# A transformer layer on one core: opening by halves, a mixer lead of two blocks, sums added ahead of weight fills

## The chip, the cores and the metric

The kernel runs on one core of one Trainium2 chip. The metric is device microseconds (us) of that core for one execution. Engines are PE (TensorE, matrix products), DVE (VectorE), ACT (ScalarE), POOL (GpSimd) and SP (SyncE, which here only issues transfers, "DMAs"). Each has its own queue of instructions and works through it in order; between engines only semaphores hold.

## The reference

One layer on 2048 tokens of width 1024, in float32: a pre-norm attention with a compressive memory over four segments of 512 tokens, and a pre-norm MLP.

```python
for s in range(N):                                   # N = 4 segments, H = 32 heads of 32
    logits = einsum("bhqd,bhkd->bhqk", qs, ks) * scale + mask
    a_dot = einsum("bhqk,bhkd->bhqd", softmax(logits), vs)
    pq = phi(qs)                                     # phi(t) = t + 1 if t > 0 else exp(t)
    num, den = einsum("bhld,bhde->bhle", pq, M), einsum("bhld,bhd->bhl", pq, z)[..., None] + 1e-6
    outs.append(g * num / den + (1.0 - g) * a_dot)   # g = sigmoid(beta), per head
    M, z = M + einsum("bhld,bhle->bhde", phi(ks), vs), z + phi(ks) summed over tokens
h = x + concat(outs) @ wo                            # q, k, v are layernorm(x) @ wq, wk, wv
out = h + gelu(layernorm(layernorm(h)) @ w1 + b1) @ w2 + b2   # w1: 1024 x 3584
```

## The kernel before

**Arithmetic.** Every float32 operand of a product is cut into a rounded high part (a copy, to the type f32r) and a low part (a subtraction); a product is three matmuls: high x high, high x low, low x high. Names end in h and l (`yh`, `yl`, `wh`, `wl`, `zh`, `zl`). The copy is nearly always on ACT, the subtraction on DVE or POOL. Tokens are worked on in two halves of 1024, each of two segments of 512 ("sl" 0 and 1).

**The run of one half.**
1. `ln1` normalises 4 tiles of 128 tokens a segment and turns them (PE transposes into `pt`, L142, L254). Its statistics come from DVE, its factors v and nb from POOL (`ln_scale`, `ln_offset`), the scaling xt from ACT. In half 0 the first segment is done by `opening` (L208 on), whose instructions are bound to the order they are written in (`in_order`), with the first weight blocks of wk, wq and wv.
2. `attention` goes over 8 groups of 4 heads and the two segments. `dense` makes keys `kps`, queries `qps` and values `vps` (L114 to L116); the four heads of the group and segment before (`heads`: scores `pqk` L497, exp L506, norm L513, transposes `ppt` L529, values `po` L549) are interleaved with it. With the first `dense` of a half, ln1 of its second segment is interleaved, so many of its steps for each step of `dense` as a ratio says.
3. The last heads run beside the first segment's product with wo (`wo_first`). Meanwhile `load_o` (L634 to L639) loads the second segment's attention outputs (`orr`) and cuts them (`oh`, `ol`), as a side run of which `PD` steps go before the first.
4. `wo_second` and `ln2` finish h and its double norm z; the normed tiles are turned. `ln2_combined` makes, from the second segment's tiles, sums and differences of token blocks (B22, T1 to T4, b12) in four steps a tile.
5. `Mixer`: the product with w1 is done by a scheme of seven products on 2x2 blocks. Its `lead` (L885 on) does, for each of 14 pairs of blocks (HP), `c1(j)`, 12 matmuls whose sum is saved as p (L896), and `c2(j)`, 12 more on top into the same bank of PSUM, of which ACT then makes gelu. Order on PE: c1(0), then for each j c1(j+1), c2(j). `begin` loads the first weights (`wx`; halves of two neighbouring blocks in one tile), which `upper` and `lower` cut on ACT and DVE. `ln2_combined` is interleaved with the lead at 0.4 of a step a PE step (3 matmuls); behind it `mp` is opened and the first weights of the pairs are fetched. Then the pairs (`Mixer.pair`, products `bps` and `dps`) are run. Both `lead` and pairs are bound to the written order.

In half 0, ln1 of half 1's first segment is interleaved with the last nine pairs, at 0.16.

**Second.** Behind half 1's pairs comes the product with w2 for all tokens, again by seven products, in jobs of 21 matmuls (`po`, L1201). For job n, `work` loads rows, makes sums (POOL), cuts the operands of job n + 2 (`prep`, L1143), and fills weight slots that are due (`fill_up`: POOL sum, ACT copy, DVE subtraction L1074). `add` then adds the product to the outputs `c` (DVE, L1211), and frees its bank.

**What sets the order.** Instructions are ordered on each engine as they are written or, outside `in_order`, by a scheduler that follows priorities from the order of writing and the dependencies. `behind`, and `add_manual_dep` with NOSYNC, hold one instruction behind another of its engine. A tile pool's tag with n buffers makes the n+1st use wait for the release of the first. PSUM has the tags d (3 banks), qk (2), pt (2) and av (1).

Of the kernel before, what the change touches and what calls it, by code (L numbers as in the profile page):

```python
# [3 lines left out]

# [21 lines left out]
NG = 8  # L26
HT = 1024
NT = HT // P
RA, RH, RS, PD, PS = 1.3, 14, 0.7, 16, 3
# [13 lines left out]
def build(tc, x, wq, wk, wv, wo, beta, w1, b1, w2, b2, out):  # L43
# [88 lines left out]
    def ln_offset(pool, m, r):  # L132
        nb = pool.tile([P, 1], F32, name="nb", bufs=4)
        nc.gpsimd.tensor_scalar(nb, m, -1.0, r, op0=ALU.mult, op1=ALU.mult)
        return nb
# [59 lines left out]
    def ln1(half, sl, delay=0):  # L195
# [8 lines left out]
        acts["y", sl] = yh, yl = seg_tiles(sl, "y")  # L204

        def take(name):
            return psum.tile([P, 512], F32, tag="av", name=name, bufs=1)

        yield from ln_tiles(lnp, xs, yh, yl, False, act=True,
                            fold=lambda src, t4: ln_transpose(lnp, src, yh, yl, t4, take))  # L210

    def opening():

        xs = [lnp.tile([P, D], F32, tag="ln", name="xt", bufs=4) for _ in range(4)]
        for t, xt in enumerate(xs):
            nc.sync.dma_start(xt, x[0, t * P:(t + 1) * P, :])
        raws, ws = {}, {}

        def load(n, w):
            raws[n] = wp.tile([P, DC, P], F32, tag="wr", name="wr", bufs=2)  # L220
            nc.sync.dma_start(raws[n], w[:, 0:P].rearrange("(c p) n -> p c n", p=P))

        def halves(n, hi_eng):
            ws[n] = [wp.tile([P, DC, P], F32R, tag=f"w{x_}", name=f"w{x_}", bufs=3) for x_ in "hl"]
            (nc.vector.tensor_copy if hi_eng == "vector" else nc.scalar.copy)(ws[n][0], raws[n])
            for k in (slice(0, 4), slice(4, 8)):
                nc.gpsimd.tensor_tensor(ws[n][1][:, k], raws[n][:, k], raw(ws[n][0])[:, k], op=ALU.subtract)
# [12 lines left out]

        def normal(t):
            m, r = scales[t][:2]
            if t < 3:
                nc.scalar.activation(xs[t], xs[t], AF.Identity, bias=scales[t][2], scale=r)
            else:
                nc.vector.tensor_scalar(xs[t], xs[t], m, r, op0=ALU.subtract, op1=ALU.mult)

        def turn(t):
            folds[t] = []
            for c in range(2):  # L250
                pt = ps_dense("pt").rearrange("p (a b) -> p a b", a=4)
                for i in range(4):
                    k = 4 * c + i
                    nc.tensor.transpose(pt[:, i, :], xs[t][:, k * P:(k + 1) * P], ident)  # L254
# [42 lines left out]
    def attention(half, first):  # L297
        ab = tc.alloc_tile_pool(name=f"ab{half}", bufs=1, reuse_waits="tile")
        acts["ab"] = ab
        mask = ab.tile([P, 512], F32, name="mask")  # L300
        quiet = behind if first else lambda op: op
        quiet(nc.gpsimd.memset(mask, 0.0))
        nc.gpsimd.affine_select(mask[:, 384:512], mask[:, 384:512], pattern=[[-1, P]],
                                compare_op=ALU.is_ge, fill=-1e9 / SCALE, base=0, channel_multiplier=1)
        mz_flat = acts["mz"] = ab.tile([P, NG * 132 + 96], F32, name="MZ")
        MZ = mz_flat[:, :NG * 132].rearrange("p (g e) -> p g e", g=NG)
        ZC = acts["mz"][:, NG * 132:NG * 133]
        if half == 0:
            quiet(nc.gpsimd.memset(mz_flat, 0.0))
        else:  # L310
            nc.sync.dma_start(mz_flat, mz_dram)
# [54 lines left out]
        def dense(g, sl, ws, u):  # L366
            s = 2 * half + sl
            behind = acts.pop("late", iter(()))
            kps = ps_dense("kps")
            for c in project(ws["k"], sl, "kps", kps):  # L370
                if c >= 2:
                    next(behind, None)
                yield
# [261 lines left out]
    def load_o(half, sl, g, tp):  # L635
        oh, ol = o_tiles(half, sl)
        orr = tp.tile([P, 512], F32, tag="tmp", name="orr", bufs=5)
        nc.sync.dma_start(orr, o_dram[2 * half + sl][g])
        split(None, orr, oh[:, g, :], ol[:, g, :], hi_eng="scalar", lo_eng="vector" if g % 2 else "gpsimd")  # L639
# [113 lines left out]
    def ln2_combined(half, hts):  # L753
# [9 lines left out]
        def fold(src, t4):  # L763
# [14 lines left out]
            def halves(name, w, lo):  # L778
                nc.scalar.copy(at[name][0], w)
                lo.tensor_tensor(at[name][1], w, raw(at[name][0]), op=sub)  # L780

# [5 lines left out]
            nc.gpsimd.tensor_tensor(t1, b12, raw(at["B11"][0]), op=sub)  # L787
            nc.gpsimd.tensor_tensor(t1, t1, raw(at["B11"][1]), op=sub)
            yield
            pt = turned(1)  # L790
            nc.scalar.copy(at["B22"][0], pt)
            nc.vector.tensor_tensor(t3, pt, b12, op=sub)
            nc.vector.tensor_tensor(at["B22"][1], pt, raw(at["B22"][0]), op=sub)
            yield
            nc.vector.tensor_tensor(t2, pt, t1, op=sub)
            nc.gpsimd.tensor_tensor(t4s, raw(at["B21"][0]), t2, op=sub)
            nc.gpsimd.tensor_tensor(t4s, t4s, raw(at["B21"][1]), op=ALU.add)
            halves("T3", t3, nc.vector)
            halves("T1", t1, nc.vector)
            yield  # L800
            halves("T2", t2, nc.vector)
            yield
            halves("T4", t4s, nc.gpsimd)
# [26 lines left out]
    class Mixer:  # L830
# [22 lines left out]
        def begin(self):  # L853
# [3 lines left out]
            def load(j):  # L857
                if j < HP:
                    raws[j] = wr = wp.tile([P, DC, P], F32, tag="wr", name="wx", bufs=2)
                    for k, b in ((0, j + 1), (4, j)):  # L860
# [4 lines left out]
            def upper(j):  # L865
                if j < HP:
                    k = slice(0, 4) if j < 0 else slice(4, 8) if j == HP - 1 else slice(0, 8)
# [9 lines left out]

            load(-1)
            load(0)
            upper(-1)  # L880
            lower(-1)
            load(1)
            self.early = load, upper, lower, left

        def lead(self):  # L885
# [19 lines left out]
            for j in (0, 1):  # L905
                upper(j)
                lower(j)
                if j == 0:
                    load(2)
            self.step = -1  # L910
            yield from c1(0)
            for j in range(HP):
# [3 lines left out]
                yield from c1(j + 1)  # L916
# [69 lines left out]
    class Second:  # L986
# [148 lines left out]
        def prep(self, n):  # L1135
            if n < len(self.jobs):
# [37 lines left out]
        def work(self, n):  # L1174
# [5 lines left out]
            self.prep(n + 2)  # L1180
            self.fill_up(n)
# [48 lines left out]
    first = opening()  # L1230
    for half in range(2):
        acts["zt"] = zt = tc.alloc_tile_pool(name=f"zt{half}", bufs=1, side="right")
        rest = attention(half, None if half else first)
# [67 lines left out]
        if half == 0:  # L1301
# [3 lines left out]
            interleave(chain(*(mixer.pair(j) for j in range(HP - 9, HP))), ln1(1, 0, 2), 0.16)  # L1305
# [4 lines left out]
        else:  # L1310
# [3 lines left out]
            for j in range(HP):  # L1314
# [3 lines left out]
                for n, _ in enumerate(mixer.pair(j)):  # L1318
# [44 lines left out]
```

## Time and profile before

| | |
|---|---|
| median of 3 runs | 2350.75 us (2349.97 to 2351.35) |
| profiled execution | 2351.56 us |
| its span in the trace | 2349.8 us |
| PE busy | 2287.8 us (97%) |
| DVE, ACT, POOL busy | 1577.1, 1231.1, 1090.0 us |
| mean granted clock of PE | 0.995 of full speed |

The span is what the trace covers; the rest of an execution's time lies around it. A row of a timeline is start, length, engine, line, operation, out<-in, shapes and number, with the idle time of the engine before it and what ended it in square brackets. Matmuls overlap in a queue, so the start-to-start step of two matmuls, not the length, is what one costs.

### The profile page before, as it was taken

The page shows a single profiled execution, that of the slowest core. Times are in us where ns is not written, and L with a number is a line of the kernel's source. Part 1 is how long each engine was busy: PE and PEld are TensorE (multiplying, and loading weights), DVE is VectorE, ACT ScalarE, POOL GpSimd, SP SyncE. Part 2 cuts the span into 40 slices and gives each one's busy share as a digit, 9 for nine tenths or more (in the row PEclk, how much of TensorE's full clock was granted, in tenths as well). Part 3 has the DMA queues.
Part 4 walks back from the last instruction along what each step waited for, and adds up shares of the span by engine and source line. Part 5 has one row for each costly group of instructions (what it writes and reads, how often), then busy time and mean ns, then how long its engine had stood idle before and what let it go on. Part 6 is the DMA issues. An engine that isn't in the chain of part 4 may idle for free.

```text
span 2349.8 us, 35272 instructions
## 1 busy us (share of the span) xinstructions
PE 2287.8 (97%) x11745; PEld 1893.0 (81%) x11745; DVE 1577.1 (67%) x3252; ACT 1231.1 (52%) x2555; POOL 1090.0 (46%) x1093
## 2 busy tenths in 40 slices
PE   7999999999999999999999999999999999999999
PEld 5888888877878887888888887878887878887887
DVE  5777777775655565777777776564566786567653
ACT  5777777775453444777777776353343223223221
POOL 4445555554253443555555545262444564155430
PEclk9999999999999999999999999999999999999999
DMA  5333333344365654433333334456567975577762
GB/s 167 98 90 91 86 85 86 88 123 161 129 192 166 193 166 136 120 85 86 86 86 86 89 103 146 142 177 196 157 178 256 353 256 189 168 241 228 251 219 93
DMA packets 322575, 355.36 MB, mean 151 GB/s; under 512 B 26174, under 2 KB 218714, under 8 KB 322394
## 3 DMA queue, kind: packets, MB, share of 16 engines
q1 hardware_dynamic: 259226, 316.40, 44.8%
q10 hardware_dynamic: 63168, 36.71, 5.2%
q8 instruction: 93, 1.52, 0.3%
q14 instruction: 88, 0.72, 0.1%
HBM read 226.59 MB, written 76.09 MB: 129 GB/s over the span
## 4 chain that ended last, share of the span: by engine, by line
PE 73%; DVE 7%; ACT 6%; DMA 5%; POOL 5%; issue 3%; SPq 0%; ACTq 0%; POOLq 0%; DVEq 0%
PE po L1201 21%; PE bps L826 8%; PE dps L826 5%; PE ppt L529 5%; PE po L549 5%; PE pqk L497 3%; PE vps L114 2%; PE vps L115 2%; PE vps L116 2%; PE kps L114 2%; PE kps L116 2%; PE kps L115 2%; PE cps L826 2%; PE qps L115 2%; PE qps L114 2%
## 5 line engine op out<-in xcount | busy, mean ns | idle before, releaser
L513 POOL TENSOR_SCALAR pr<-pr,nm,gate 128x128 f32<-128x128 f32 (+3 forms) x512 | 321.6, 637 | 361.9 <-DVE nm L510 286.1
L506 ACT ACTIVATE pr<-pr,mx 128x256 f32<-128x256 f32 (+3 forms) x512 | 287.6, 562 | 162.5 <-DVE mx L498 159.6
L536 DVE TENSOR_TENSOR ptl<-ppt,pth 128x512 fp32r<-128x512 f32 (+1 forms) x384 | 227.6, 600 | 77.9 <-ACT pth L531 72.9
L498 DVE CUSTOM_DVE_ANT_0 pr<-pqk,mask 128x256 f32<-128x256 f32 (+3 forms) x512 | 243.0, 484 | 38.6 <-PE pqk L497 36.4
L529 PE MATMUL ppt<-ident,pr 128*128 128x128 f32 x1280 | 223.5, 277 | 5.8 <-DMA orr<-o_dram 3.8
L531 ACT CAST pth<-ppt 128x512 fp32r<-128x512 f32 (+1 forms) x384 | 194.1, 517 | 37.6 <-PE ppt L529 31.5
L1211 DVE TENSOR_TENSOR c<-c,po 128x512 f32<-128x512 f32 x160 | 105.4, 683 | 143.8 <-PE po L1201 143.5
L529 PEld LDWEIGHTS ppt<-ident,pr 128*128 128x128 f32 x1280 | 164.2, 140 | 37.2 <-DVE ptl L536 6.4
L91 POOL TENSOR_TENSOR wl<-wr,wh 128x1024 fp32r<-128x1024 f32 x53 | 126.9, 2394 | 87.3 <-DVE wh L88 33.6
L497 PE MATMUL pqk<-ks,qs 96*128 96x256 f32 (+3 forms) x512 | 161.8, 316 | 0.5 <-DVE mx L498 0.5
L549 PE MATMUL po<-ptl,vs 128*64 128x512 f32 (+3 forms) x512 | 154.9, 312 | 4.6 <-DVE ptl L536 4.4
L549 PE MATMUL po<-pth,vs 128*64 128x512 f32 (+3 forms) x512 | 156.8, 328 | 1.5 <-ACT pth L531 1.5
L1201 PE MATMUL po<-w2h,zh 128*128 128x512 f32 x378 | 120.8, 389 | 0.0
L934 POOL TENSOR_TENSOR s<-r 128x512 f32<-128x512 f32 x28 | 42.6, 1520 | 160.7 <-DVE sa L950 102.6
L497 PEld LDWEIGHTS pqk<-ks,qs 96*128 96x128 f32 x512 | 96.4, 188 | 22.3 <-DVE mx L498 0.9
L1071 POOL TENSOR_TENSOR w2r<-w2r 128x512 f32<-128x512 f32 x54 | 88.7, 1654 | 54.3 <-DMA w2r<-in_B_w 36.3
L826 PE MATMUL bps<-zh,sa 128*128 128x512 f32 x336 | 110.8, 391 | 1.6 <-DVE u L964 1.6
L826 PE MATMUL bps<-zh,sb 128*128 128x512 f32 x336 | 110.9, 391 | 0.9 <-DVE u L976 0.9
L114 PE MATMUL kps<-yh,wh 128*128 128x512 f32 x256 | 108.5, 424 | 0.9 <-ACT yh L144 0.8
L114 PE MATMUL vps<-yh,wh 128*128 128x512 f32 x256 | 108.9, 426 | 0.2 <-ACT omt L479 0.2
L114 PE MATMUL qps<-yh,wh 128*128 128x512 f32 x256 | 107.7, 421 | 0.0
L1201 PE MATMUL po<-w2h,hl 128*128 128x512 f32 x322 | 103.0, 389 | 2.5 <-DVE c L1211 2.5
(237 smaller groups left out, 6700.7 us busy)
## 6 DMA issues: line engine op xcount, KB each, us to landing
hr<-h_dram SPq DMA_DIRECT2D x112, 448.0 KB, 5.1
w2r<-in_B_w SPq DMA_DIRECT2D x122, 256.0 KB, 4.2
r<-in_B_w SPq DMA_DIRECT2D x56, 512.0 KB, 4.2
h_dram<-ht ACTq DMA_DIRECT2D x84, 256.0 KB, 3.7
ks<-kh SPq DMA_DIRECT2D x256, 64.0 KB, 2.0
qs<-qh SPq DMA_DIRECT2D x256, 64.0 KB, 2.0
wr<-in_A_wo SPq DMA_DIRECT2D x32, 512.0 KB, 3.9
wx<-in_B_w SPq DMA_DIRECT2D x56, 256.0 KB, 3.9
```

What stands on the lines that cost most here:

```text
L114: nc.tensor.matmul(ps, ah, bh, start=first, stop=False)
L115: nc.tensor.matmul(ps, ah, bl, start=False, stop=False)
L497: nc.tensor.matmul(pqk[:, :n], u["qs"][j][:, i * P:(i + 1) * P], u["ks"][j][:, 0:n], start=True, stop=True)
L498: nc.vector.tensor_tensor_reduce(out=st["pr"][:, offs[i]:offs[i] + n], in0=pqk[:, :n], in1=mask[:, 512 - n:512], op0=ALU.add, op1=ALU.min, ...
L506: nc.scalar.activation(pi, pi, AF.Exp, bias=mx[:, i:i + 1], scale=-1.0, accum_out=mx[:, 4 + i:5 + i])
L513: nc.gpsimd.tensor_scalar(pi, pi, nm[:, 4 + k:5 + k], gate[:, 1, 4 * g + j:4 * g + j + 1], op0=ALU.mult, op1=ALU.mult)
L529: nc.tensor.transpose(ppt[:, o:o + P], pr[:, offs[i] + jk * P:offs[i] + (jk + 1) * P], ident)
L531: nc.scalar.copy(pth[:, base:base + w], ppt[:, :w])
L536: nc.vector.tensor_tensor(o, x0, x1, op=ALU.subtract)
L549: nc.tensor.matmul(po[:, P * jk:], v, st[part][:, koff[jk]:koff[jk] + w], start=(jk, part) == (0, "pth"), stop=(jk, part) == (2, "ptl"))
L826: nc.tensor.matmul(ps, x_[:, c, :], y_[:, c, :], start=first and c == 0 and n == 0, stop=last and c == 3 and n == 2, skip_group_check=True)
L1201: nc.tensor.matmul(ps, x_[:, k], y_[k], start=opens and k == 0 and i == 0, stop=closes and k == self.KP - 1 and i == 2, skip_group_check=True)
```

## The change

- Opening: the attention pool, with the memsets of its mask and of MZ, is made before it. Tile 0 of x is loaded in two halves. The transposes use the banks of qk and pt. The first key block `kps` is made in `opening`, in two halves of 256 tokens (`keys`), the first six of the first half's eight steps before the last tile is turned. POOL's second half of q's low part, wv's load and v's low part go into ln1 (`rest`, by `aside`), v's held behind POOL's nb. ln1 of the second segment runs at 1.6 instead of 1.1.
- `load_o` of the second segment: the copy oh is held behind the last matmul written, and `PD` is 20 instead of 16.
- `ln2_combined` takes six steps a tile instead of four, and its first subtraction of t1 goes from POOL to DVE, which reads PSUM.
- `lead` runs c1 two blocks ahead of c2, and loads and cuts accordingly.
- ln1 of half 1's second segment is begun in the last pairs of half 0 (its first three steps), at 0.17 instead of 0.16.
- In `Second`, `add` of job n goes ahead of `fill_up`, and the operands of job 2 are cut in the last pair.

```diff
-RA, RH, RS, PD, PS = 1.3, 14, 0.7, 16, 3
+RA, RH, RS, PD, PS = 1.3, 14, 0.7, 20, 3
-        nc.gpsimd.tensor_scalar(nb, m, -1.0, r, op0=ALU.mult, op1=ALU.mult)
+        acts["nb"] = nc.gpsimd.tensor_scalar(nb, m, -1.0, r, op0=ALU.mult, op1=ALU.mult)
...
     def opening():
-        for t, xt in enumerate(xs):
-            nc.sync.dma_start(xt, x[0, t * P:(t + 1) * P, :])
+        for k in (slice(0, 512), slice(512, 1024)):
+            nc.sync.dma_start(xs[0][:, k], x[0, 0:P, k])
+        for t in range(1, 4):
+            nc.sync.dma_start(xs[t], x[0, t * P:(t + 1) * P, :])
...
-                pt = ps_dense("pt").rearrange("p (a b) -> p a b", a=4)
+                pt = psum.tile([P, 512], F32, tag=("qk", "pt")[c], name="pt", bufs=2).rearrange("p (a b) -> p a b", a=4)
...
+        kps = ws["kps"] = ps_dense("kps")
+
+        def keys(i, cs):
+            n = slice(256 * i, 256 * i + 256)
+            for c in cs:
+                mm3(kps[:, n], ws["k"][0][:, c, :], ws["k"][1][:, c, :], yh[:, c, n], yl[:, c, n], c == 0, c == DC - 1)
...
-            halves("k", "vector")
+            upper("k", "vector")
+            under("k", 0)
+            under("k", 1)
             turn(1)
             lower(1, 0)
             normal(3)
             turn(2)
             lower(2, 0)
+            keys(0, range(6))
             turn(3)
             lower(3, 0)
             lower(3, 1)
-            halves("q", "scalar")
-            load("v", wv)
-            halves("v", "scalar")
+            keys(0, range(6, DC))
+            upper("q", "scalar")
+            under("q", 0)
+            keys(1, range(DC))
+
+        def rest(t):
+            if t == 0:
+                under("q", 1)
+                load("v", wv)
+                upper("v", "scalar")
+            elif t < 3:
+                tc.add_manual_dep(under("v", t - 1).ins, acts["nb"].ins.name, NOSYNC, reason="program order")
...
-                    interleave(d, ln1(half, 1), 1.1)
+                    interleave(d, acts.pop("ahead") if half else ln1(0, 1, aside=ws.pop("rest")), 1.1 if half else 1.6)
...
-        split(None, orr, oh[:, g, :], ol[:, g, :], hi_eng="scalar", lo_eng="vector" if g % 2 else "gpsimd")
+        hi, lo = oh[:, g, :], ol[:, g, :]
+        op = nc.scalar.copy(hi, orr)
+        if sl == 1:
+            tc.add_manual_dep(op.ins, acts["mm"].ins.name, NOSYNC, reason="program order")
+        (nc.vector if g % 2 else nc.gpsimd).tensor_tensor(lo, orr, raw(hi), op=ALU.subtract)
...
-            nc.gpsimd.tensor_tensor(t1, b12, raw(at["B11"][0]), op=sub)
+            nc.vector.tensor_tensor(t1, pt, raw(at["B11"][0]), op=sub)
+            yield
             nc.gpsimd.tensor_tensor(t1, t1, raw(at["B11"][1]), op=sub)
-            yield
             pt = turned(1)
...
-                    h, l, _ = left[j - 1]
+                    h, l, _ = left[j - 2]
...
-                yield from c1(j + 1)
+                yield from c1(j + 2)
                 lower(j + 2)
                 yield from c2(j)
...
             self.prep(n + 2)
+            self.add(*got)
             self.fill_up(n)
...
-                got = self.product(n)
-                self.work(n)
-                self.add(*got)
+                self.work(n, self.product(n))
...
-            interleave(chain(*(mixer.pair(j) for j in range(HP - 9, HP))), ln1(1, 0, 2), 0.16)
+            acts["ahead"] = ln1(1, 1)
+            interleave(chain(*(mixer.pair(j) for j in range(HP - 9, HP))),
+                       chain(ln1(1, 0, 2), islice(acts["ahead"], 3)), 0.17)
...
+                    if (j, n) == (HP - 1, 14):
+                        second.prep(2)
```

More of the change, by code (lines that the diff above doesn't have):

```diff
@@ L3 @@
 from functools import partial
+from itertools import islice
 import concourse.bass as bass
@@ L193, in seg_tiles, with ln1 @@
         return h, l
-    def ln1(half, sl, delay=0):
+    def ln1(half, sl, delay=0, aside=None):
         xs = []
@@ L295, in load_block, with attention_pool, attention @@
         return wh, wl
[L297 to L302, printed above, removed]
+    def attention_pool(half):
+        ab = acts["ab"] = tc.alloc_tile_pool(name=f"ab{half}", bufs=1, reuse_waits="tile")
+        mask = acts["mask"] = ab.tile([P, 512], F32, name="mask")
+        nc.gpsimd.memset(mask, 0.0)
         nc.gpsimd.affine_select(mask[:, 384:512], mask[:, 384:512], pattern=[[-1, P]],
                                 compare_op=ALU.is_ge, fill=-1e9 / SCALE, base=0, channel_multiplier=1)
-        mz_flat = acts["mz"] = ab.tile([P, NG * 132 + 96], F32, name="MZ")
-        MZ = mz_flat[:, :NG * 132].rearrange("p (g e) -> p g e", g=NG)
+        acts["mz"] = ab.tile([P, NG * 132 + 96], F32, name="MZ")
+        if half == 0:
+            nc.gpsimd.memset(acts["mz"], 0.0)
+        else:
+            nc.sync.dma_start(acts["mz"], mz_dram)
+    def attention(half, first):
+        ab, mask = acts["ab"], acts["mask"]
+        MZ = acts["mz"][:, :NG * 132].rearrange("p (g e) -> p g e", g=NG)
         ZC = acts["mz"][:, NG * 132:NG * 133]
[L308 to L311, printed above, removed]
         def tmp(name):
@@ L368, in dense @@
             behind = acts.pop("late", iter(()))
[L369 to L372, printed above, removed]
-                yield
+            kps = ws.pop("kps", None)
+            if kps is None:
+                kps = ps_dense("kps")
+                for c in project(ws["k"], sl, "kps", kps):
+                    if c >= 2:
+                        next(behind, None)
+                    yield
             kh, kl = tmpr("kh"), tmpr("kl")
@@ L776, in turned @@
                 return pt
-            def halves(name, w, lo):
-                nc.scalar.copy(at[name][0], w)
-                lo.tensor_tensor(at[name][1], w, raw(at[name][0]), op=sub)
+            hi = lambda name, w: nc.scalar.copy(at[name][0], w)
+            lo = lambda name, w, eng: eng.tensor_tensor(at[name][1], w, raw(at[name][0]), op=sub)
             b12, t1 = pair("b12t1")
@@ L859, in load @@
                     raws[j] = wr = wp.tile([P, DC, P], F32, tag="wr", name="wx", bufs=2)
[L860 removed]
+                    for k, b in ((0, j + 2), (4, j)):
                         if 0 <= b < HP:
@@ L903, in c2 @@
                 self.out(j, 0, ps)
-            for j in (0, 1):
+            for j in (-1, 0):
                 upper(j)
                 lower(j)
-                if j == 0:
-                    load(2)
+                load(j + 2)
             self.step = -1
             yield from c1(0)
+            left.pop(-2)
+            upper(1)
+            yield from c1(1)
+            left.pop(-1)
+            lower(1)
             for j in range(HP):
@@ L1135, in prep @@
         def prep(self, n):
-            if n < len(self.jobs):
+            if n < len(self.jobs) and n not in self.hl:
                 src, b = self.srcs.pop(self.jobs[n])
@@ L1172, in ahead, with work @@
                         self.out(*self.at(p, w))
-        def work(self, n):
+        def work(self, n, got):
             late, self.later = self.later, []
@@ L1228, in zx_tile @@
         return acts["zt" if n == 3 else "zx"].tile([P, 4, 512], F32R, tag=f"t{x_}{n}", name=f"z{x_}{n}")
-    first = opening()
     for half in range(2):
         acts["zt"] = zt = tc.alloc_tile_pool(name=f"zt{half}", bufs=1, side="right")
-        rest = attention(half, None if half else first)
+        attention_pool(half)
+        first = None if half else opening()
+        rest = attention(half, first)
         hts = [lnp.tile([P, D], F32, tag="ln", name="ht0", bufs=4) for _ in range(4)]
```

47 lines of the change are left out of this document (29 added, 18 removed).

## The prediction

> **What bounds the kernel now.** I read the page's totals first, the waits of PE second, the granted clock in short windows third, and the instructions around each wait last.
>
> ```profile
> span 2349.8 us, 35272 instructions
> PE 2287.8 (97%) x11745; PEld 1893.0 (81%) x11745; DVE 1577.1 (67%) x3252; ACT 1231.1 (52%) x2555; POOL 1090.0 (46%) x1093
> ```
>
> PE is the bound: it is busy 2287.8 of 2349.8 us and no other engine passes 67%. The change leaves the multiplications as they are, so it can win only the 62 us in which PE stands still, and whatever PE does slowly. The waits of PE name the first:
>
> ```profile
> PE pt L254 <- ACT xt L244: 8.5, 1, 8.5
> PE cps L826 <- ACT p L896: 7.9, 7, 2.8
> PE po L1201 <- DVE c L1211: 7.9, 3, 3.3
> PE pt L142 <- ACT xt L163: 7.1, 2, 5.2
> PE ppt L529 <- DMA orr<-o_dram: 3.8, 1, 3.8
> PE cps L826 <- DVE wl L876: 1.3, 2, 0.7
> ```
>
> The columns are total us, number, longest. The 8.5 at L254 is the load and norm of the first tokens, which stays. The other five make 28.0 us, all at places that the change touches. Slow work is the second part. In these windows (start:end, length, busy time of PE, PEld, DVE, ACT and POOL, granted clock, DMA share, GB/s) PE is busy at about half clock behind a wait:
>
> ```profile
> 30.00:34.00 4.00, 4.00 (x14) 3.03 (x13) 1.29 (x2) 2.20 (x3) 0.26 (x1) 0.54 0.22 51
> 536.00:538.00 2.00, 1.56 (x4) 0.71 (x3) 2.00 (x6) 1.98 (x7) 1.27 (x2) 0.50 0.71 244
> 540.00:542.00 2.00, 2.00 (x10) 1.80 (x9) 1.91 (x5) 1.28 (x4) 1.17 (x4) 0.50 0.00 0
> 676.00:680.00 4.00, 4.00 (x13) 3.21 (x12) 4.00 (x3) 2.96 (x5) 3.11 (x2) 0.65 0.30 85
> 1566.00:1570.00 4.00, 4.00 (x12) 3.12 (x11) 4.00 (x3) 3.02 (x5) 3.19 (x3) 0.57 0.36 112
> 924.00:928.00 4.00, 4.00 (x15) 3.08 (x14) 1.52 (x3) 3.08 (x4) 2.73 (x9) 0.57 0.62 209
> 1816.00:1818.00 2.00, 1.14 (x5) 0.99 (x6) 2.00 (x4) 0.07 (x1) 0.00 (x0) 1.00 0.78 215
> ```
>
> A window costs its length times one minus its clock: 1.8 us at 30, 3.0 over 536 to 542, 1.4, 1.7 and 1.7 at 676, 1566 and 924. That is 9.6 us. The last row shows that not every wait brings it (the 3.3 us wait for c ends at 1816.9, at full clock). So 37.6 us lie open, and beside them what the opening could start earlier.
>
> **Opening.**
>
> ```profile
> 16.90 0.50 PE L114 MATMUL kps<-yh,wh 128*128 128x512 f32 x1
> 23.02 0.39 PE L114 MATMUL qps<-yh,wh 128*128 128x512 f32 x1
> 28.84 1.12 PE L142 MATMUL pt<-ident,xt 128*128 128x128 f32 x4 [5.21 <-ACT xt L163]
> 18.47 2.54 POOL L227 TENSOR_TENSOR wl<-wr,wh 128x512 fp32r<-128x512 f32 x2 [4.11 <-ACT wh L225]
> 21.30 2.53 POOL L227 TENSOR_TENSOR wl<-wr,wh 128x512 fp32r<-128x512 f32 x2 [0.28 <-ACT wh L225]
> 23.77 0.53 POOL L302 MEMSET mask<- 128x512 f32 x1
> 24.23 1.06 POOL L309 MEMSET MZ<- 128x1152 f32 x1
> 27.24 0.51 POOL L134 TENSOR_SCALAR nb<-mv,v 128x1 f32<-128x1 f32 x2
> 154.22 0.28 PE L497 MATMUL pqk<-ks,qs 96*128 96x256 f32 x1
> 154.33 0.40 PE L114 MATMUL qps<-yh,wh 128*128 128x512 f32 x1
> 154.57 0.40 PE L115 MATMUL qps<-yl,wh 128*128 128x512 f32 x1
> ```
>
> The 24 key matmuls run from 16.90 to 23.02, because they wait for all four token tiles. The change makes them 48 of 256 columns. A 256-column matmul holds PE from 154.22 to 154.33, 0.11 us, and one of 512 from 154.33 to 154.57, 0.24 (0.23 on the mean of a long run), so the halves cost nothing in sum (24 x 0.11 = 2.6 us each). Eighteen of the first half's run before tile 3 is turned, in PE's present gaps; behind the folded last tile, at about 16.9 us, stand 6 + 24 matmuls, 3.4 us. The queries then start near 20.4 instead of 23.0: 2.6 us won. [...]
>
> POOL today does two weights' low halves (5.1 us of work from 18.47 to 23.8) and both memsets before the norm's factors nb at 27.24, and PE waits 5.21 us for the normalised xt. Afterwards the memsets come first, when POOL has little to do, and the second half of q and all of v go between and behind the nb's. nb then needs only q's first half (1.27 us, from 18.5) and its own steps: near 22, with xt normalised at 23.5. PE still meets three small waits there, which I put at 3.5 us together by following the new order on ACT and DVE (an estimate from the durations quoted), so 1.7 of 5.2 is won. The slow window goes: 1.8. Sum 6.1; I take 6. Ends: 3 (the new waits are as long as the old one), 8.5 (they and the rest of the waits go). The two loads of tile 0 count nothing: its statistics need both halves. On SP the wv load and ln1's tile loads change places with nothing that is waited for.
>
> **o loads held back (the later order of orr and oh).**
>
> ```profile
> 529.79 0.62 ACT L90 CAST oh<-orr 128x512 fp32r<-128x512 f32 x1 [3.41 <-DMA orr<-o_dram]
> 525.05 1.92 SPq L638 DMA_DIRECT2D orr<-o_dram  x4
> 534.38 0.44 PE L529 MATMUL ppt<-ident,pr 128*128 128x128 f32 x2 [3.79 <-DMA orr<-o_dram]
> ```
>
> ACT stands 3.41 us before a copy of orr, whose load SP issued at 525.05 behind wo's weights; behind it wait an exp and the copy of ppt, and PE stands 3.79. In the new order the first copy comes 20 ACT instructions later, behind those, some 10 us on. Its added order edge is behind a matmul already queued, and what stands behind it on ACT is the next head's exp, by then with its data loaded. I take the whole wait and its slow window, 3.8 + 3.0 = 6.8, rounded 7. Lower end 3.5: the wait returns by half at a later copy. Half 1 shows no such wait, and gains nothing.
>
> **Mixer lead and combined operands.**
>
> ```profile
> 674.67 0.50 PE L826 MATMUL cps<-zh,wh 128*128 128x512 f32 x1 [2.77 <-ACT p L896]
> 673.51 0.62 ACT L779 CAST zh<-b12t 128x512 fp32r<-128x512 f32 x1 [0.17 <-POOL b12t L788]
> L787 POOL TENSOR_TENSOR b12t<-b12t,zh 128x512 f32<-128x512 f32 x4 | 5.6, 1408 | 0.9 <-ACT b12t L786 0.9
> L795 DVE TENSOR_TENSOR t2t<-pt,b12t 128x512 f32<-128x512 f32 x3 | 2.1, 687 | 4.2 <-POOL b12t L788 4.2
> ```
>
> Today c2(j) needs the p copy of c1(j), and one product (c1(j+1), 12 matmuls of 0.23, 2.7 us) stands between them. ACT makes the p copy in its order, behind casts that wait for POOL (the cast at 673.51). With c1(j+2) ahead, three products, 8.2 us, cover the same copy, and each weight pair is due one block later. The waits of cps for p (7.9) and wl (1.3) should go, with the slow windows at 676 and 1566 (1.4 + 1.7): 12.3 in both halves. Against that, an extra half-size cast and subtraction per half beside PE's own start, and a bank must be free two blocks earlier: gelu of j-2, behind the same ACT queue, has some 5.4 us (two products) before PE needs it. Six steps a token move t1's first subtraction from POOL (1.41 us, 4 a half) to DVE from PSUM (0.69, the nearest row) and spread the work over 24 steps at 0.4 a PE step, 60 instead of 40 PE steps of 0.7 us; the first fetch for the pairs then falls three blocks later and has still four to spare. Cost nothing while DVE stays below PE. I take 11; ends 5 (the bank wait takes the place of half of it) and 13.
>
> **ln1 of half 1, begun in the last pair.**
>
> ```profile
> 922.44 2.52 ACT L163 ACTIVATE xt<-xt,nb,v 128x1024 f32<-128x1024 f32 x2 [3.17 <-POOL nb L134]
> 923.74 0.66 PE L142 MATMUL pt<-ident,xt 128*128 128x128 f32 x4 [1.88 <-ACT xt L163]
> 918.73 2.41 POOL L91 TENSOR_TENSOR wl<-wr,wh 128x1024 fp32r<-128x1024 f32 x1 [0.31 <-ACT wh L90]
> ```
>
> The first of the four tiles is normalised before the half ends: 1.88 and the 1.7 of the window at 924 go. But the next two tiles' nb stay behind v's low half on POOL (918.73 to 921.1, a nb each 1.3 us after), and the new ACT order has their norms ahead of the first fold's yh copy, so I expect a new PE wait of about 2.1. Net 1.5. Ends: -1 (with a slow window of its own), +4. SP loads the next half's x tiles ahead of MZ; MZ is read only after q and v products.
>
> **Second: products added ahead of the fills.**
>
> ```profile
> 1816.86 0.47 PE L1201 MATMUL po<-zh,zl 128*128 128x512 f32 x1 [3.28 <-DVE c L1211]
> 1895.82 0.47 PE L1201 MATMUL po<-w2h,hl 128*128 128x512 f32 x1 [2.52 <-DVE c L1211]
> 1889.98 5.10 DVE L1074 TENSOR_TENSOR w2l<-w2r,w2h 128x512 fp32r<-128x512 f32 x2
> 1895.00 0.67 DVE L1211 TENSOR_TENSOR c<-c,po 128x512 f32<-128x512 f32 x1
> ```
>
> The second of these waits is an add behind two fills of 2.55 us, and so is the third (7.9 - 3.28 - 2.52 = 2.1); the first is an add behind prep(2), which now is made in the last pair. With the add first, the fills run while the next product does. What they hold up next is prep(n+3), due two products on (21 matmuls, 4.8 us each). I take 2 + 1.3 + 1 = 4.3 of 7.9, since the later fills will be felt by the next prep; ends 1 and 7.5.
>
> **Sum.** 6 + 7 + 11 + 1.5 + 4.3 = 29.8. The profiled execution took 2351.56, 1.8 more than its span and 0.8 more than the median, which is what the runs will show: 2350.75 - 29.8 = 2321. All low ends give 11.5 (2339), all high ends 40 (2311).
>
> **Rivals.**
> Waits move: each cover that I counted on is gone for half of the gain, since the same ACT and DVE queues feed the next thing (the lead's bank release, opening's three waits). For it speaks that ACT's p copy waited for POOL's slow work, which is only spread; against it, that no engine but PE is above 67% busy. Gain 15: 2336.
> Slower: DVE in Second. The add now waits in DVE's queue for the product's end, and the fills run behind it. There are 12 changes of the weight slots; if the last fill of each came late by its whole 2.55 us, that is 31, against 25.5 from the other parts: 2356. It decides from 2.1 us a change. Against it: a fill is due two jobs ahead, 9.6 us.
> Clock: short new waits keep half-clock stretches. The 1.88 us wait brought one of 1.7, the 3.28 none; if three new waits (opening twice, half 1) bring 2 each, 2327. [...]
> The change not taking effect: the order edges are there in the instruction order; under 0.02.
>
> **How the numbers follow.** Likeliest (2321, own range 2314 to 2329) 0.55; clock 0.13; waits move 0.22; slower or no change 0.08; more won than all but the high ends 0.02. The range of 8 in 10: 2310 to 2338. Faster 0.92, within 0.2% (4.7 us, what a measurement can tell) 0.03, slower 0.05.
>
> **What would show it.** Right: key matmuls from about 13.5 us, no wait above 2 us before 50 us; no wait on orr; cps' wait for p under 2 us in sum and full clock at 670 to 680 and 1562 to 1570; a start of half 1 with a wait of about 2 us; po's waits for c about half. PE idle near 42 us instead of 62 and a mean clock near 1. Wrong: a wait of cps for ACT ht, of po for DVE w2l or prep, new windows at half clock, or a Second that takes longer than before.

## The result, and the profile after

The changed kernel takes 2322.54 us (median of 4 runs, 2321.96 to 2323.11) against 2350.78 for the kernel before on the same chip (4 runs): a ratio of 0.988, 95% interval 0.9863 to 0.9897, or 28.2 us less. The forecast was 2321 with 2314 to 2329 as its own range. The total is right; several of its terms are not, as the stages below show.

The page and the waits of PE, of the changed kernel:

```profile
span 2321.3 us, 35329 instructions
PE 2278.3 (98%) x11769; PEld 1891.7 (81%) x11769; DVE 1554.7 (67%) x3262; ACT 1229.1 (53%) x2557; POOL 1070.1 (46%) x1085
PE pt L265 <- ACT xt L255: 9.8, 2, 8.6
PE pt L143 <- DVE yl L147: 5.9, 4, 2.5
PE pwo L115 <- DVE zl L147: 3.7, 4, 1.6
PE po L1249 <- DVE c L1259: 1.5, 2, 1.3
PE po L1249 <- DVE hl L1190: 0.9, 2, 0.5
PE po L1249 <- DVE zh L1190: 0.4, 1, 0.4
```

PE's idle time fell from 62 to 43 us. The waits of cps for p and wl are gone, and those for orr, and the waits for c are down from 7.9 to 1.5. New are the wait of pt for DVE yl, 5.9 us, and in Second small ones for the cuts of a next job's operands (hl, zh), 1.3 us. To see which stage won what, the span is cut at the same matmuls in both kernels (the start of the n-th matmul of a name). The windows below are the opening (to the first values of the second segment), wo's first segment, and the lead, in half 0; length, busy times, clock as before. Of the kernel before:

```profile
0.00:64.31 64.31, 48.03 (x240) 38.20 (x240) 38.42 (x95) 34.59 (x66) 28.62 (x54) 0.95 0.58 171
512.20:584.26 72.06, 66.23 (x340) 53.60 (x339) 45.33 (x104) 39.37 (x81) 37.36 (x39) 0.95 0.46 152
633.34:723.46 90.12, 85.83 (x381) 69.21 (x380) 48.20 (x47) 48.08 (x72) 40.40 (x29) 0.98 0.62 187
```

Of the changed kernel:

```profile
0.00:63.22 63.22, 48.75 (x264) 40.77 (x265) 39.36 (x95) 33.95 (x66) 28.41 (x54) 0.97 0.60 173
510.87:576.20 65.33, 63.23 (x341) 51.90 (x339) 45.25 (x103) 39.45 (x81) 36.20 (x37) 1.00 0.49 165
626.65:709.35 82.70, 82.70 (x382) 68.49 (x380) 49.31 (x52) 48.52 (x73) 36.05 (x25) 1.00 0.68 207
```

The opening is only 1.1 us shorter, though it ought to have been 6. The lead is 7.4 us shorter and PE is busy in all of it. The span by these cuts up to the end of the last matmul, in us, with most of the runs that the next section tells of:

| stage | before | changed | e1 old opening | e2 lead of one | e3 four steps | e4 old o loads | e7 two banks | e9 pace alone | e11 three banks |
|---|---|---|---|---|---|---|---|---|---|
| opening | 64.3 | 63.2 | 64.1 | 63.2 | 62.3 | 63.5 | 57.5 | 63.2 | 56.9 |
| attention, half 0 | 447.9 | 447.7 | 447.9 | 447.7 | 447.7 | 447.7 | 447.9 | 448.0 | 447.9 |
| wo, first segment | 72.1 | 65.3 | 65.3 | 65.4 | 65.4 | 70.5 | 65.4 | 69.0 | 65.3 |
| wo, second segment | 49.1 | 50.5 | 49.9 | 50.1 | 49.6 | 49.0 | 50.0 | 50.1 | 49.9 |
| lead, half 0 | 90.1 | 82.7 | 82.7 | 82.7 | 90.4 | 82.7 | 82.7 | 82.8 | 82.7 |
| pairs and start of half 1 | 237.6 | 236.6 | 237.3 | 237.0 | 237.9 | 236.6 | 234.9 | 236.1 | 234.8 |
| attention, half 1 | 445.0 | 446.0 | 445.0 | 445.9 | 445.6 | 446.0 | 444.9 | 445.1 | 446.0 |
| wo, first segment | 67.1 | 64.2 | 65.7 | 64.2 | 65.7 | 67.3 | 64.2 | 67.2 | 64.1 |
| wo, second segment | 49.3 | 50.3 | 49.9 | 50.3 | 51.2 | 48.7 | 50.6 | 49.3 | 50.3 |
| lead, half 1 | 91.2 | 82.7 | 82.7 | 82.7 | 90.4 | 82.7 | 82.7 | 82.8 | 82.7 |
| pairs, half 1 | 190.2 | 190.3 | 190.2 | 190.2 | 190.2 | 190.5 | 190.3 | 190.3 | 190.3 |
| Second, to its first late job | 13.0 | 11.0 | 11.3 | 11.4 | 11.0 | 10.8 | 10.9 | 13.1 | 11.1 |
| Second, the rest | 529.0 | 527.1 | 527.3 | 527.4 | 529.5 | 529.2 | 529.6 | 530.1 | 526.6 |

The two leads won 15.9 us of the 28, wo's stages 7.3 net of the second segment (9.7 less 2.4), Second 3.9, the opening 1.1, the rest about nothing. The expectations below end half 1's lead about 1 us later, at another matmul, hence their 83.6, 91.5, 92.3 and 16.1.

### The profile page after: what moved, and what is told of

Read it like the earlier page. It is cut to its first block, busy times and chain, and to the rows that moved or that the text cites. A ratio compares the mean times of both kernels' runs of the same rounds, so it can differ in the third digit from the quotient of the medians.

```text
span 2321.3 us, 35329 instructions
## 1 busy us (share of the span) xinstructions
PE 2278.3 (98%) x11769; PEld 1891.7 (81%) x11769; DVE 1554.7 (67%) x3262; ACT 1229.1 (53%) x2557; POOL 1070.1 (46%) x1085
## 4 chain that ended last, share of the span: by engine, by line
PE 77%; DVE 6%; ACT 6%; DMA 4%; POOL 4%; issue 3%; SPq 0%; ACTq 0%; POOLq 0%; DVEq 0%
PE po L1249 19%; PE bps L869 9%; PE cps L869 6%; PE dps L869 6%; PE ppt L564 5%; PE po L584 5%; PE pqk L532 3%; PE vps L115 2%; PE vps L116 2%; PE vps L117 2%; PE kps L115 2%; PE kps L117 2%; PE kps L116 2%; ACT pr L541 2%; PE qps L115 1%
## 5 line engine op out<-in xcount | busy, mean ns | idle before, releaser
L1118 POOL TENSOR_TENSOR w2r<-w2r 128x512 f32<-128x512 f32 x54 | 83.6, 1560 | 63.0 <-DMA w2r<-in_B_w 33.4
L115 PE MATMUL kps<-yh,wh 128*128 128x512 f32 (+1 forms) x264 | 110.6, 419 | 0.4 <-ACT yh L145 0.4
## 6 DMA issues: line engine op xcount, KB each, us to landing
hr<-h_dram SPq DMA_DIRECT2D x112, 448.0 KB, 5.2
```

The source lines that it names most:

```text
L115: nc.tensor.matmul(ps, ah, bh, start=first, stop=False)
```

## The experiments

All but e9 start from the changed kernel. The times, each with the ratio to the kernel before on its chip (its interval, where there are several runs; the others are single runs): e1 2324.34 (0.9863 to 0.9911), e2 2323.9 (0.9862 to 0.991), e3 2339.46 (0.9945 to 0.9971), e4 2329.91 (0.988 to 0.9937), e5 2324.13, e6 2325.5, e7 2318.13 (0.9843 to 0.9876), e8 2327.18, e9 2333.59 (0.9909 to 0.9941), e10 2326.0, e11 2314.06 (0.9827 to 0.9862), e12 2325.21. Where one part is told of, its stage in the trace is what is compared; the totals carry a spread of 2 to 3 us from Second, whose last row differs between runs of kernels that are alike there.

**e2: lead of one block, six steps kept.**

```diff
         def lead(self):
-                    h, l, _ = left[j - 2]
+                    h, l, _ = left[j - 1]
...
-                yield from c1(j + 2)
+                yield from c1(j + 1)
```

> The changed kernel with the lead of one block (begin and lead of before), the combined operands still in six steps. Theory A (the lead of two blocks is what removes the waits of cps for p; the two leads won 16.1 us together): 10 to 14 us longer, 2332 to 2336. Theory B (the six steps, with the first subtraction on DVE, do it, since the p copy waited on ACT behind casts that waited for POOL): under 4 us longer.

Both leads stayed at 82.7 us. Theory A, which was my prediction's, fell at once. With the six steps, two blocks of lead win nothing that can be seen.

**e3: four steps, lead of two blocks kept.**

```diff
         def fold(src, t4):
-            nc.vector.tensor_tensor(t1, pt, raw(at["B11"][0]), op=sub)
-            yield
+            nc.gpsimd.tensor_tensor(t1, b12, raw(at["B11"][0]), op=sub)
             nc.gpsimd.tensor_tensor(t1, t1, raw(at["B11"][1]), op=sub)
+            yield
...
+            halves("T3", t3, nc.vector)
+            halves("T1", t1, nc.vector)
+            yield
+            halves("T2", t2, nc.vector)
+            yield
+            halves("T4", t4s, nc.gpsimd)
```

> The changed kernel with the combined operands in four steps again, the lead of two blocks kept. Theory A (the lead covers the waits alone): within 2 us of the changed kernel, no wait of cps for p above 0.5. Theory B (the six steps do it): 8 to 14 us longer, with waits of cps for p back in both leads.

Both leads are back at 90.4, though with two blocks of lead. What changes is only the name of the wait. Waits of PE, then PE, ACT and POOL around the longest of them, in e3:

```profile
PE cps L865 <- ACT ht L882: 8.0, 4, 3.8
PE cps L865 <- DVE wl L915: 2.7, 2, 1.4
667.66 0.80 PE L865 MATMUL cps<-zh,wh 128*128 128x512 f32 x1 [3.84 <-ACT ht L882]
666.40 0.62 ACT L818 CAST zh<-b12t 128x512 fp32r<-128x512 f32 x1 [1.37 <-POOL b12t L827]
666.92 0.68 ACT L882 ACTIVATE ht<-cps,b1c 128x512 f32<-128x512 f32 x1
657.59 1.67 POOL L835 TENSOR_TENSOR t<-zh,t2t 128x512 f32<-128x512 f32 x1 [0.80 <-DVE t2t L834]
659.33 1.62 POOL L836 TENSOR_TENSOR t<-t,zl 128x512 f32<-128x512 f32 x1
661.69 2.10 POOL L819 TENSOR_TENSOR zl<-t,zh 128x512 fp32r<-128x512 f32 x1 [0.73 <-ACT zh L818]
663.75 1.27 POOL L826 TENSOR_TENSOR b12t<-b12t,zh 128x512 f32<-128x512 f32 x1
665.10 1.26 POOL L827 TENSOR_TENSOR b12t<-b12t,zl 128x512 f32<-128x512 f32 x1
667.17 1.66 POOL L835 TENSOR_TENSOR t<-zh,t2t 128x512 f32<-128x512 f32 x1 [0.80 <-DVE t2t L834]
```

Before, PE waited for the p copy; now it waits for the bank that gelu (ht) frees. Here as there, what PE waits for stands on ACT behind a cast that waits for POOL (the one at 666.40). POOL's round for one token tile takes 9.6 us (657.59 to 667.17), of which 7.9 are work (1.67 + 1.62 + 2.10 + 1.27 + 1.26). Four steps at 0.4 a PE step ask for a tile every 10 PE steps of 0.69 us, 6.9 us. So POOL falls behind, and whatever follows its consumers on ACT falls behind with it, with a lead of two blocks as with one.

**e5 and e6: pace and engine apart.** e5 has four steps at a slower pace; e6 has six steps, with t1's first subtraction on POOL.

```diff
         for _ in mixer.lead():
-            acc += 0.4
+            acc += 0.267
```

> The changed kernel with the combined operands in four steps, but 0.267 of a step for each PE step instead of 0.4, so that they take as many PE steps as six do at 0.4. Each lead took 82.7 and 83.6 us with six steps, 90.4 and 91.5 with four, whichever the lead. Theory A (pace: POOL's share of the lead's first 40 us was too large): leads of 83 to 85 us. Theory B (it is t1's first subtraction on POOL, 1.4 us of each token's chain, and the order of ACT's casts, not the pace): leads of 87 to 91 us.

```diff
-            nc.vector.tensor_tensor(t1, pt, raw(at["B11"][0]), op=sub)
+            nc.gpsimd.tensor_tensor(t1, b12, raw(at["B11"][0]), op=sub)
```

> The changed kernel in six steps at 0.4, with t1's first subtraction on POOL again. Theory A (pace): leads of 83 to 85 us. Theory B (the subtraction's engine): 87 to 91 us. If both this and the slow four steps come near 83, each of the two suffices.

Each lead is 82.77 us in e5 and 82.70 in e6. The pace alone suffices: at 0.267, or six steps at 0.4, a tile is asked for every 15 PE steps, 10.3 us, above POOL's 9.6. The subtraction's engine does not matter.

**e9: the pace alone, in the kernel before.** The same one number is changed (0.4 to 0.267), and nothing else of the change is there.

> The kernel before with one number changed: the combined operands go into the lead at 0.267 of a step for each PE step instead of 0.4. Lead of one block, four steps, nothing else of the change. Theory A (the pace alone carried both leads): leads of 83 to 84 us instead of 90.1 and 92.3, time 2333 to 2336. Theory B (pace and one of lead or six steps are needed together): leads of 86 us or more, 2340 or more.

Theory A. Windows of the lead in half 0, of e9 and then of e3:

```profile
630.25:713.03 82.78, 82.78 (x382) 68.46 (x380) 46.95 (x47) 48.10 (x72) 41.57 (x29) 1.00 0.69 204
```

```profile
624.97:715.38 90.41, 85.03 (x381) 69.17 (x380) 49.48 (x48) 49.03 (x73) 43.67 (x29) 0.98 0.64 189
```

One number wins 15.7 us in the two leads. In the time it wins 15.1 us by the medians (2348.72 on its chip to 2333.59), and 14 to 21 by the interval of the ratio. The lead of two blocks and the six steps with their moved subtraction add nothing to it.

**e1: the old opening.** `opening` and the place of the memsets are those of before, and ln1 of the second segment runs at 1.1 without the weights' steps.

```diff
         attention_pool(half)
-        first = None if half else opening()
...
-                    interleave(d, acts.pop("ahead") if half else ln1(0, 1, aside=ws.pop("rest")), 1.1 if half else 1.6)
+                    interleave(d, acts.pop("ahead") if half else ln1(0, 1), 1.1)
```

> The changed kernel with the opening, the place of the attention pool and the ratio 1.1 of the kernel before; all other parts kept. Theory A (the opening's gain is given back by 52 us, because the second segment's folds, one PSUM bank and about 2.06 us each, set when its keys can start): span 1 to 2 us longer than the changed kernel, 2322.5 to 2323.5. Theory B (the opening wins its 6 us, and something else in the stage loses 5): about 6 us longer, 2327 to 2328.

The stretch is 64.1 us, 0.9 longer than with the new opening: theory A. (With the same opening code the stretch varies from profile to profile: 61.8 to 63.5 in the eight with the new opening and one bank, 63.2 to 64.3 in the three with the old, so the size of 0.9 is within that spread.) In the changed kernel, PE in the opening and ACT's copies of ln1's second-segment folds:

```profile
15.46 0.56 PE L115 MATMUL kps<-yh,wh 128*128 128x256 f32 x1
23.45 0.40 PE L115 MATMUL qps<-yh,wh 128*128 128x512 f32 x1
31.48 0.66 PE L143 MATMUL pt<-ident,xt 128*128 128x128 f32 x4 [2.05 <-DVE yl L147]
42.63 0.66 PE L143 MATMUL pt<-ident,xt 128*128 128x128 f32 x4 [1.22 <-DVE yl L147]
44.08 0.50 PE L115 MATMUL kps<-yh,wh 128*128 128x512 f32 x1 [0.38 <-ACT yh L145]
35.09 0.59 ACT L145 CAST yh<-pt 128x512 fp32r<-128x512 f32 x1 [0.86 <-PE pt L143]
37.15 0.59 ACT L145 CAST yh<-pt 128x512 fp32r<-128x512 f32 x1 [0.99 <-PE pt L143]
39.21 0.59 ACT L145 CAST yh<-pt 128x512 fp32r<-128x512 f32 x1 [1.48 <-PE pt L143]
41.27 0.58 ACT L145 CAST yh<-pt 128x512 fp32r<-128x512 f32 x1 [0.22 <-PE pt L143]
```

Four copies in a row stand 2.06 us apart: turn on PE, copy on ACT, subtraction on DVE, and then only the next turn, because all folds use the one bank av. Eight folds at that step take some 16 us (an estimate, 8 x 2.06); the eight turns run from 26.49 to 45.77, and the second segment's first keys at 44.08 wait for the copy of the seventh. Counted in columns of matmuls done, the changed kernel led the one before by 7.0 us at 28 us, by 4.8 at 40, and by 1.0 at 52.

**e7 and e11: two and three banks for the folds.** The edit is that of e11; e7 takes av and pt in turn.

```diff
         def take(name):
-            return psum.tile([P, 512], F32, tag="av", name=name, bufs=1)
+            turns.append(name)
+            tag, bufs = (("av", 1), ("pt", 2), ("qk", 2))[len(turns) % 3]
+            return psum.tile([P, 512], F32, tag=tag, name=name, bufs=bufs)
+
+        turns = []
```

> The changed kernel with ln1's second-segment transposes in turn in the banks av and pt, in both halves, instead of in av alone. Theory A (the folds' cycle through one bank, 2.06 us a fold, gates the second segment's keys and gave the opening's gain back): the waits of pt for DVE yl (5.9 us) and the half clock at 44 to 48 go, and the time falls by 4 to 7 us, to 2316 to 2319. Theory B (the norm chain of POOL, ACT and the x loads gates it): under 1.5 us.

> The changed kernel with ln1's transposes in turn in the banks av, pt and qk. Theory A (the bank cycle is still what gates the folds with two): the opening stretch 2 us or more shorter than with two banks (57.45), 2315 to 2316.5. Theory B (two banks do; then the norm chain and DVE gate): within 1 us of the run with two banks, 2317 to 2319.

The opening took 57.5 us with two banks and 56.9 with three; the start of half 1 gained too (236.6 to 234.9 and 234.8). The second segment's first keys start at 39.57 in e7 and at 39.04 in e11, instead of 44.08. Changed kernel, then e7 and e11, the window of the slow stretch:

```profile
44.00:48.00 4.00, 3.92 (x16) 3.38 (x17) 3.33 (x13) 3.45 (x12) 2.24 (x4) 0.60 1.02 349
```

```profile
44.00:48.00 4.00, 4.00 (x24) 3.39 (x22) 2.56 (x9) 2.42 (x9) 2.25 (x3) 1.00 0.33 124
```

```profile
44.00:48.00 4.00, 4.00 (x25) 3.46 (x24) 2.57 (x11) 2.56 (x8) 2.78 (x3) 1.00 0.73 237
```

The half clock is gone in both. The time of e7 is as theory A had it. Of the waits, e7 keeps one, at the third fold:

```profile
29.91 0.66 PE L143 MATMUL pt<-ident,xt 128*128 128x128 f32 x4 [1.81 <-DVE yl L147]
```

e11 has none of them. By the stretch e11 goes with its theory B; its time is below the range of either theory. Whether two banks are enough for the opening is open: e11's stretch is only 0.5 us shorter, but its tile 1 of x came 1.5 us later than e7's (DVE's statistics of it start at 8.13 and 6.60). e11 has the lowest time of this study: 2314.06 us, ratio 0.9845 (0.9827 to 0.9862). That is just ahead of the changed kernel's interval (from 0.9863) and overlaps e7's. In the profiles e11 is 2.8 us ahead of e7, and Second's rest alone makes 3.0.

**e12: the old opening with two banks.** The edits of e1 and e7 together.

> The kernel with the opening of before (first run) and the two banks for ln1's transposes. Theory A (with the folds' cycle gone the new opening is worth its 6 us): opening stretch near 63, against 57.45 with the new opening and two banks. Theory B (the two banks alone carry it): near 58 to 59.

The stretch is 63.78 us: theory A. So the opening alone wins 0.9, the banks alone 0.4 (64.14 to 63.78), and both together 6.7. The first two are within the spread of profiles named above, the third is far outside it. Each hides behind the other. In e12 the wait that is left is that of the old opening:

```profile
29.25 1.97 PE L143 MATMUL pt<-ident,xt 128*128 128x128 f32 x8 [4.80 <-ACT xt L164]
```

**e4: the old o loads.**

```diff
-RA, RH, RS, PD, PS = 1.3, 14, 0.7, 20, 3
+RA, RH, RS, PD, PS = 1.3, 14, 0.7, 16, 3
...
-        if sl == 1:
-            tc.add_manual_dep(op.ins, acts["mm"].ins.name, NOSYNC, reason="program order")
```

> The changed kernel with PD = 16 and without the order edge of oh behind a matmul. Theory A: the stage of wo's first segment in half 0 is 7 us longer, with the wait of ppt for the DMA of orr and the half clock back, half 1 unchanged: 2328 to 2329. Theory B (half 1's stage, 67.1 to 64.2 us between the kernels, won by the same edit): 9 to 10 us longer in both halves, and the stage after it, wo's second segment, 1 us shorter in each half: 2330.

Nearer to theory B: wo's first segment is 5.2 us longer in half 0 and 3.1 in half 1, 8.3 in place of 9 to 10, and the second segment is 1.4 and 1.7 shorter. ACT waits again at its head (e4):

```profile
528.12 0.62 ACT L675 CAST oh<-orr 128x512 fp32r<-128x512 f32 x1 [2.76 <-DMA orr<-o_dram]
531.53 0.44 PE L564 MATMUL ppt<-ident,pr 128*128 128x128 f32 x2 [2.02 <-DVE ptl L571]
```

The edit is worth 5.2 us net, over both halves. What it wins in the first segment it partly gives back in the second. In the changed kernel:

```profile
595.94 0.49 PE L115 MATMUL pwo<-zh,oh 128*128 128x512 f32 x1 [1.50 <-DVE zl L147]
591.90 0.62 ACT L913 CAST wh<-wx 128x512 fp32r<-128x512 f32 x1 [1.41 <-DMA wx<-in_B_w]
```

PE starts a new output pwo there, and waits for DVE's subtraction at L147, which frees a bank of tag d from a turned tile of ln2. ACT's copy of that tile stands behind the cast at 591.90, which waits for the mixer's first weights. Counted from the start of the second segment, that cast comes 1.4 us later than in e4 (15.7 against 14.3 us). This is read from the rows; no run changes that order alone. In half 1 the first segment takes 67.1 to 67.3 us in the three profiles without the edit, and with it 64.1 to 64.7, or 65.6 to 65.7 (e1, e3 and four more).

**e8 and e10: the adds, and ln1 begun early.** e8 puts the add behind the fills again; e10 does not begin ln1 of the second segment in the last pairs.

```diff
-            self.add(*got)
             self.fill_up(n)
...
-                self.work(n, self.product(n))
+                got = self.product(n)
+                self.work(n, got)
+                self.add(*got)
```

> The changed kernel with the add behind the fills again, the operands of job 2 still cut in the last pair. Theory A (the order is what removes the waits at the 16th job and in the second half): the two waits of po for c, 2.5 and 2.1 us, return, 2326 to 2327. Theory B (only the start's early cut counts, 2.0 of 3.7): within 1 us of the changed kernel.

```diff
-                       chain(ln1(1, 0, 2), islice(acts["ahead"], 3)), 0.17)
+                       ln1(1, 0, 2), 0.16)
```

> The changed kernel, but ln1 of half 1's second segment is not begun in half 0's last pairs (0.16 again). Theory A (that part won 1.3 us at the start of half 1): that stretch 1 to 2 us longer, with the wait of pt for ACT xt of 1.9 and half clock back. Theory B (it won nothing): same stretch within 0.5.

e8, and then e10:

```profile
1873.88 0.47 PE L1248 MATMUL po<-w2h,hl 128*128 128x512 f32 x1 [3.64 <-DVE c L1258]
```

```profile
910.57 0.66 PE L143 MATMUL pt<-ident,xt 128*128 128x128 f32 x4 [1.88 <-ACT xt L164]
```

In e8 the wait at the 16th job is back (3.64), the one in the second half is not; Second's rest takes 529.0 us, against 526.6 to 529.6, mean 527.9, in the eleven profiles that have the new order, and 529.0 and 530.1 in the two of the old (before and e9). So the order is worth about 1.5 us by these means, and the ranges overlap: not settled. That job 2 is cut early is plain: 13.0 and 13.1 us without, 10.4 to 11.5 with it. In e10 the stretch of pairs and start is 236.0 us, against 236.6 to 238.0 in the eight profiles with one bank that begin ln1 early, and 237.6 and 236.1 in the two of before's kind. Theory B: that part won nothing. In e10 and the changed kernel, both at a granted clock of 1.00 from 905 to 921 us, the stretch takes 236.0 and 236.6. The early begin exchanged the wait for xt, 1.88, for one for yl (2.50 in the changed kernel), which frees the bank av. That e10's time is 3.5 us above the changed kernel's comes mostly from elsewhere: both second segments of wo together are 3.0 us longer, and the mean granted clock of its profile is 0.998 against 0.999.

## Why the prediction was right, and where it was not

**The sum** came out at 28.2 against 29.8 by luck: two errors of five us, in the opening and the lead, cancelled.

**Opening (6, measured 1.1).** Two steps failed. The first is "The queries then start near 20.4": they started at 23.45, and the keys at 15.46, not 13.5, since tile 1 came later. "The two loads of tile 0 count nothing" does not hold up. DVE's statistics of tile 1, before and changed:

```profile
5.85 1.23 DVE L121 BATCH_NORM_STATS2 st<-xt 128x6 f32<-128x512 f32 x2
```

```profile
7.61 1.29 DVE L122 BATCH_NORM_STATS2 st<-xt 128x6 f32<-128x512 f32 x2 [1.68 <-DMA xt<-in_A_x]
```

They start 1.8 us later and wait for the load, in a kernel whose only change ahead of them is the split load and the memsets. All ten profiles with the split load have such a wait and start them at 6.60 to 8.21 us; the four with one load have none and start them at 5.85 to 5.97. No run parts the split from the place of the memsets. The keys follow: they start at 13.70 in e7, where tile 1 came first, and at 16.07 in e2, where it came last. And the first nine key matmuls of 256 columns ran 0.21 us apart, not 0.12, at a granted clock of 1.00. In e4 it is the same, in the other eight profiles not; why is open.

The other failed step is "three small waits, 3.5 us together". They were 3.8, but I had taken them for leftovers of the norm chain; they are waits for the one bank of the folds. The second fold met it still held at 31.48, since ACT and DVE had other work before the first fold's copy and subtraction (28.91 and 30.74, for a turn at 26.49); from 34.40 to 42.63 the turns came every 2.06 us. Behind these waits stands a half-clock window (0.60 at 44 to 48, against 1.00 in e7 and e11), which I had only under the rival of the clock. That the 256-column halves cost nothing held from the tenth on: they step by 0.12 us (17.52 to 18.47) at a granted clock of 1.00, half of the 0.23 of 512 columns (the queries from 23.45 on).

**o loads (7, measured 5 to 7).** Wait and slow window went as said (the clock over the stage is 1.00, before 0.95); the first segment of half 0 took 72.1, 70.5 and 69.0 us in the three profiles without the edit, 65.3 with it. Wrong is "Half 1 shows no such wait, and gains nothing": its stage is up to 3 us longer without the edit. Missed, too, is what comes next: the bank that PE waits for in wo's second segment, 2.4 us over both halves. These two also nearly cancel.

**Lead (11, measured 15.9).** The failed step is "With c1(j+2) ahead, three products, 8.2 us, cover the same copy". It does not help (e2, e3). What I had costed "at nothing", the spreading from 40 to 60 PE steps, is all of it (e5, e9). My own warning, a wait of cps for ht, is what the lead of two shows when the pace is too high (e3). The surplus over the 12.3 counted lay in PE's busy time: 85.83 us in the first lead and 86.09 in the second, against 82.70 for the same matmuls. The slow windows (clocks of 0.65 at 676 and 0.57 at 1566) explain 1.4 and 1.7 of that; the rest is open.

**ln1 early (1.5, measured nothing)** by the new wait that I had expected, at 2.5 instead of 2.1. **Second (4.3, measured 3.9)**: 2.0 for the early cut, as said; the order of the adds 1.5, within the noise. Part of what fell away in the waits for c came back as waits for the cuts of a next job's operands, which I had named as a sign of being wrong: 1.3 us here, and about 2 us at once in e3, e4 and e10.

**The rivals.** The slower one did not happen: PE waited once for a fill, 0.2 us. "Waits move" did, in the opening, at the start of half 1, in wo's second segment and a little in Second. The clock: one new slow window of 1.7 us, for three expected.

## What to carry to other kernels

When work is interleaved into a stage, compare its pace with the longest round of any engine it uses, waits between engines included: here 6.9 us asked against 9.6 needed, and a lead of two blocks covered a queue that falls further behind at every tile no better than a lead of one (90.4 us in e3, 90.1 before). When a start is made earlier, look at the next gate in the same stretch before counting the gain: two changes that alone were worth 0.9 and 0.4 us, within the spread of profiles, were worth 6.7 together. Where a total comes out right, check the stages all the same.

## What the hardware showed that I had not expected

A half-clock stretch again followed short waits: in the changed kernel only one stretch is slow, 44 to 48 us (0.60), behind waits of 1.22 and 0.38 us, while those of 2.05 and 2.50 us at 31 and 913 brought none. Windows of the changed kernel behind these two:

```profile
31.00:35.00 4.00, 3.35 (x20) 2.70 (x21) 1.71 (x3) 2.33 (x4) 1.35 (x4) 1.00 0.44 100
913.00:917.00 4.00, 3.94 (x21) 3.26 (x22) 1.42 (x4) 3.22 (x5) 0.00 (x0) 1.00 0.71 236
```

Nor does the place decide it. In e8, whose code is the same up to Second, the same wait of 2.50 us was followed by half clock. The wait in the changed kernel, then the wait and the window behind it in e8:

```profile
913.06 0.66 PE L143 MATMUL pt<-ident,xt 128*128 128x128 f32 x4 [2.50 <-DVE yl L147]
```

```profile
911.96 0.66 PE L143 MATMUL pt<-ident,xt 128*128 128x128 f32 x4 [2.50 <-DVE yl L147]
913.00:917.00 4.00, 4.00 (x14) 3.22 (x13) 2.22 (x5) 3.20 (x5) 0.68 (x2) 0.57 0.53 140
```

So in these profiles neither the length of one wait (1.22 us before a clock of 0.60, 2.50 before one of 1.00) nor the code around it (2.50 us in both kernels, then 1.00 and 0.57) told whether the clock would drop. What makes it drop, no run shows.
